# Layer one in fp32 for its first three tiles, experts' weights split two ahead, and their rows turned by TensorE

## The chip, the cores and the metric

The kernel runs on one core of one Trainium2 chip. The metric is the device time of the whole launch in microseconds. Matrix products run on TensorE (PE in the profile, its weight loads PEld), element-wise work on VectorE (DVE), ScalarE (ACT) and GpSimd (POOL), and most DMAs are issued by SyncE's queue (SP), some by GpSimd's.

## What is computed

Windowed attention feeds a two-layer block, and its result feeds eight experts with a greedy assignment of tokens. All inputs are given as float64. Cut to what matters:

```python
scores = scale * q @ k.T                  # (4, 8, 576, 64), window of 64 keys
attn = softmax(where(mask, scores, -1e9))
x = rearrange(attn @ v)                   # 2304 tokens x 512

h = x @ w_in                              # 512 x 2048: "layer one"
g = where(h > 0, h, exp(min(h, 0)) - 1)   # ELU
x = g @ w_out                             # 2048 x 512: "layer two"

logits = x @ w_gate                       # 8 experts
# all 2304 x 8 logits in falling order: a token goes to the first expert
# that still has room; each expert takes exactly 288 tokens
out[mask_e] = maximum(x[mask_e] @ w1[e], 0) @ w2[e]   # 512 -> 1024 -> 512
```

## The kernel before

Most products need more than f16 gives, so an operand is **split**: `hi` is its f16 rounding, `lo` the f16 of the rest, and a product of two split operands is three f16 products (hi hi, hi lo, lo hi). The attention's products and the transposes run in fp32.

The weights W_in and W_out come as float64. `to32` (L103) joins the two 32-bit halves with three integer operations on VectorE (L106 to L108) into a float32, and then splits it: ScalarE writes `hi` and VectorE `lo` (L115, L116), or, in every other call, ScalarE scales and writes `hi`, and GpSimd `lo` (L111 to L113). `prep_win` (L140) does that for W_in in 16 pieces into `wi`, `prep_wout` for W_out in 16 pieces.

Attention goes in 18 chunks of 128 tokens. `att_s1` turns q and k by TensorE, `att_s2` makes the scores, `att_soft` the exponentials and their normalising (L289, one GpSimd operation per half chunk), `att_s3` turns the result, and `att_s4` multiplies by v: L303 takes `vn`, the chunk's own rows, and `vp`, rows shifted by 64. `vp` is written by GpSimd (L241, L243) for chunks 0 to 5, and loaded once more from HBM for the rest (L222, L223). `att_out` puts the result, split (L315 ScalarE, L316 VectorE), into `xt`, the input of layer one.

Layer one runs over seven tiles of 256, 256, 256, 256, 512, 512 and 256 tokens (`layer1`, L361). A step takes 512 results: for tiles of 256 tokens that is 2 x 12 products of 256 columns (L377). ELU is then a chain: ScalarE relu and exp (L381, L382), GpSimd (L383), VectorE with the accumulator (L384), GpSimd `hi` (L386), VectorE `lo` (L387; on GpSimd in tile 0). The three accumulator banks `mm` come free with L384. Layer two (`layer2`, L434) takes 48 products of 512 columns for 128 tokens. Streams are interleaved by `weave` with estimated weights, and the framework's scheduler then orders each engine's instructions by a timeline of its own. Layer one of tiles 0 to 2, attention's first chunks and the preparing of both weights come first; layer two of tile 0 starts after them.

From about 440 us the routing runs, a chain of small steps between VectorE and TensorE in seven phases. Its TensorE instructions are pinned in program order, and between them stand products of layer two of tiles 4, 5 and 6 as a filling: the table `W` says how many at which step (`W[7]` and `W[8]` once per phase, `W[15]` once ahead of the first phase, whose first product is L599).

Then the experts run one after the other. Expert e has 96 + 96 products of 288 columns (L864, L899) on 288 tokens, which GpSimd gathers and SP's transposing DMAs turn (`xet`). ScalarE writes `hi` of the first products (`finish`, L869), VectorE `lo` (L870). The weights of expert e come in four pieces of 1 MB (`raw`, three buffers, SP). `split_expert` splits them: `hi` on ScalarE (L769) and GpSimd (L771), `lo` on VectorE (L772). Experts 0 and 1 are split during routing, expert e + 1 during expert e from e = 1 on. The results leave split into `oh` (`leave`), three DMA transposes per expert on SP turn them (`rt`, L826), ScalarE and VectorE join them to `orow`, and GpSimd scatters the rows to the output. Only the last expert is turned by TensorE (`last_rows`, L851).

Of the kernel before, what the change touches and what calls it, by code (L numbers as in the profile page):

```python
# [39 lines left out]
def attention_moe_moe2_kernel(ctx: ExitStack, tc: tile.TileContext, q, k, v, w_in, w_out, w_gate, w1, w2, out):  # L40
# [119 lines left out]
    def prep_wout(j):  # L160
        for f in range(4 * j, 4 * j + 4):
# [6 lines left out]
            to32(st, 64.0, w[:, 0, i], w[:, 1, i], f % 2 == 0)  # L168
# [56 lines left out]
    CV = 6  # L225

    def att_s1(c):
# [12 lines left out]
        elif c < CV:  # L240
            nc.gpsimd.tensor_scalar(VP[c][64:], V[c - 1][64:], 1.0, 1.0, op0=OP.mult, op1=OP.mult)  # L241
        if c < CV:
            nc.gpsimd.tensor_scalar(VP[c][:64], V[c][:64], 1.0, 1.0, op0=OP.mult, op1=OP.mult)  # L243
# [33 lines left out]
    def att_soft(c):  # L277
# [10 lines left out]
        for blk in range(2):  # L288
            nc.gpsimd.tensor_tensor(P[c, blk], P[c, blk], rs[:, blk, :, None].to_broadcast([128, ND, 128]), op=OP.mult)  # L289
# [71 lines left out]
    def layer1(t, pools=None):  # L361
# [5 lines left out]
        for f in range(0, NF, nf):  # L367
# [12 lines left out]
            r = work.tile([128, nf, n], F32, name="r", bufs=3)  # L380
# [660 lines left out]
```

## Time and profile before

| what | us |
|---|---|
| median of three timed runs | 840.78 (839.29 to 842.84) |
| profiled execution | 838.07 |
| its span | 836.4 |
| TensorE busy in the span | 749.8 (90%) |
| VectorE busy | 454.6 (54%) |
| ScalarE busy | 342.2 (41%) |
| GpSimd busy | 362.2 (43%) |

The profile shows one execution. A busy share is a mean over stages with different limits, so the span is read in stages: 0 to 39 the first loads and chunks, 39 to 169 layer one of tiles 0 to 2 with attention and both weights, 169 to 440 layer two and the rest of attention and layer one, 440 to 603 routing, and from there the experts. A timeline row's length of a run of products runs to the end of its last, which overlaps the next row; spacing is read from the starts.

### The profile page before, as it was taken

How to read it: one execution, taken by the hardware profiler on the slowest of the kernel's cores; microseconds unless marked ns; L12 is line 12 of the kernel's file. 1: busy time of each engine (PE TensorE's matmuls, PEld its weight loads, DVE VectorE, ACT ScalarE, POOL GpSimd, SP SyncE). 2: the span in 40 equal slices, each digit the busy share in tenths (PEclk: the TensorE clock that was granted, in tenths of full speed). 3: DMA queues.
4: the chain of work that ended last, by engine and by line, in shares of the span. 5: the costliest groups of instructions: out<-in, count | busy, mean ns of one | idle time of the engine just before them, and what ended most of it. 6: DMA issues, size and time to landing. Idle time of an engine off the chain costs nothing.

```text
span 836.4 us, 16758 instructions
## 1 busy us (share of the span) xinstructions
PE 749.8 (90%) x6742; PEld 489.7 (59%) x6742; DVE 454.6 (54%) x980; ACT 342.2 (41%) x847; POOL 362.2 (43%) x474
## 2 busy tenths in 40 slices
PE   7578878899999999999997899798879988898996
PEld 5466666645685456555583344343457766676786
DVE  4777899821164115455546655756613675457550
ACT  4666556524454246644446611301112234333332
POOL 7357475623242124575447522825061444433321
PEclk9799889999999999999998999999989999999998
DMA  9956364405456536010104220400044789988831
GB/s 238 309 122 171 96 151 138 90 1 127 102 102 121 108 92 87 1 52 1 44 14 162 99 77 18 171 14 13 25 116 90 228 211 272 254 238 187 255 89 39
DMA packets 156669, 98.82 MB, mean 118 GB/s; under 512 B 135600, under 2 KB 135600, under 8 KB 156592
## 3 DMA queue, kind: packets, MB, share of 16 engines
q1 hardware_dynamic: 153520, 88.31, 41.9%
q0 software_dynamic: 3072, 9.44, 3.9%
q8 instruction: 53, 0.87, 0.4%
q14 instruction: 24, 0.20, 0.1%
HBM read 72.37 MB, written 9.44 MB: 98 GB/s over the span
## 4 chain that ended last, share of the span: by engine, by line
PE 49%; DVE 22%; DMA 11%; issue 7%; ACT 4%; POOL 3%; SPq 3%; POOLq 0%; ACTq 0%; DVEq 0%
PE ps_mm L434 19%; PE ps_mm L377 16%; DMA raw<-in_moe_w_dram 7%; PE ps_mm L864 3%; DVE b L107 2%; DVE slab L772 2%; DVE b L106 2%; DMA out_dram<-orow,idx 2%; DVE b L108 2%; ACT sm L284 2%; PE ps_pv L303 2%; DVE r L384 1%; PE ps_sc L599 1%; DVE ge L596 1%; SPq L208 1%
## 5 line engine op out<-in xcount | busy, mean ns | idle before, releaser
L377 PE MATMUL ps_mm<-xt,slab 128*128 128x256 f16 (+1 forms) x1344 | 207.1, 313 | 15.4 <-DVE r L384 12.8
L434 PE MATMUL ps_mm<-slab,g 128*128 128x512 f16 x864 | 216.4, 384 | 0.0
L377 PEld LDWEIGHTS <-slab 128*128 128x128 f16 x1344 | 132.1, 101 | 74.1 <-issue 15.2
L434 PEld LDWEIGHTS <-g 128*128 128x128 f16 x864 | 74.5, 99 | 75.9 <-issue 8.5
L864 PE MATMUL ps_mm<-xet,slab 128*128 128x288 f16 (+1 forms) x840 | 104.2, 282 | 7.8 <-DVE h L870 7.0
L864 PEld LDWEIGHTS <-slab 128*128 128x128 f16 x840 | 77.9, 100 | 29.9 <-issue 9.9
L899 PEld LDWEIGHTS <-slab 128*128 128x128 f16 x960 | 79.1, 98 | 27.3 <-issue 10.2
L899 PE MATMUL ps_sc<-h,slab 128*128 128x288 f16 (+1 forms) x480 | 72.8, 263 | 9.1 <-ACT h L869 9.1
L381 ACT ACTIVATE r<-ps_mm 128x512 f32<-128x512 f32 x72 | 42.9, 598 | 90.7 <-PE ps_mm L377 59.8
L384 DVE TENSOR_TENSOR r<-ps_mm,r 128x512 f32<-128x512 f32 x72 | 49.6, 689 | 53.1 <-POOL r L383 53.0
L383 POOL TENSOR_SCALAR r<-r 128x512 f32<-128x512 f32 x72 | 53.7, 746 | 54.3 <-ACT r L382 49.9
L289 POOL TENSOR_TENSOR sm<-sm,rs 128x512 f32<-128x512 f32 x36 | 39.8, 1126 | 86.1 <-DVE rs L287 41.2
L386 POOL TENSOR_SCALAR g<-r 128x512 f16<-128x512 f32 x72 | 50.5, 702 | 57.2 <-DVE r L384 38.9
L899 PE MATMUL ps_tp<-h,slab 128*128 128x288 f16 (+1 forms) x480 | 71.7, 263 | 0.0
L772 DVE SCALAR_TENSOR_TENSOR slab<-raw,slab 128x512 f16<-128x512 f32 x96 | 64.5, 706 | 7.7 <-ACT slab L769 4.0
L387 DVE TENSOR_TENSOR g<-r,g 128x512 f16<-128x512 f32 x64 | 46.6, 729 | 38.9 <-POOL g L386 38.5
L816 POOL DMA_INDIRECT out_dram<-orow,idx x24 | 31.9, 1329 | 73.2 <-DVE orow L839 57.1
L284 ACT ACTIVATE sm<-ps_sc,mx 128x128 f32<-128x128 f32 x144 | 50.8, 378 | 26.1 <-DVE mx L282 26.1
L769 ACT ACTIVATE slab<-raw 128x512 f16<-128x512 f32 x48 | 27.5, 621 | 73.6 <-DMA raw<-in_moe_w_dram 72.7
L447 POOL TENSOR_TENSOR xs<-r,xs 128x512 f16<-128x512 f32 x17 | 21.0, 1233 | 68.1 <-ACT xs L446 68.1
L445 ACT ACTIVATE r<-ps_mm 128x512 f32<-128x512 f32 x17 | 10.2, 601 | 98.1 <-PE ps_mm L434 98.1
L771 POOL TENSOR_SCALAR slab<-raw 128x512 f16<-128x512 f32 x48 | 29.7, 633 | 43.2 <-DMA raw<-in_moe_w_dram 38.0
(212 smaller groups left out, 1145.6 us busy)
## 6 DMA issues: line engine op xcount, KB each, us to landing
raw<-in_moe_w_dram SPq DMA_DIRECT2D x32, 1024.0 KB, 5.4
slab<-in_moe_w_in_dram SPq DMA_DIRECT2D x16, 512.0 KB, 7.2
st<-in_moe_w_out_dram SPq DMA_DIRECT2D x16, 512.0 KB, 4.6
x2d<-xs SPq DMA_DIRECT2D x18, 256.0 KB, 2.1
qn<-in_q_dram SPq DMA_DIRECT2D x16, 256.0 KB, 6.5
kn<-in_k_dram SPq DMA_DIRECT2D x16, 256.0 KB, 6.1
vn<-in_v_dram SPq DMA_DIRECT2D x16, 256.0 KB, 4.9
vp<-in_v_dram SPq DMA_DIRECT2D x24, 128.0 KB, 3.1
```

Of the source, the lines that this page charges most:

```text
L284: nc.scalar.activation(P[c, blk][:, i], SC[blk][:, i], AF.Exp, bias=mx[:, blk, i:i + 1], accum_out=rs[:, blk, i:i + 1])
L289: nc.gpsimd.tensor_tensor(P[c, blk], P[c, blk], rs[:, blk, :, None].to_broadcast([128, ND, 128]), op=OP.mult)
L377: nc.tensor.matmul(ph[:, i], wi[d, (f + i) // 8][:, a, (f + i) % 8 * 128:((f + i) % 8 + 1) * 128], XT[t][:, b, d, :n], start=m == 0, stop= ...
L381: nc.scalar.activation(r, ph, AF.Relu, scale=-1.0 / A_H)
L383: nc.gpsimd.tensor_scalar(r, r, -1.0, A_H, op0=OP.add, op1=OP.mult)
L384: nc.vector.tensor_tensor(r, ph, r, op=OP.max)
L386: last["pool"] = nc.gpsimd.tensor_scalar(hi, r, 1.0, 1.0, op0=OP.mult, op1=OP.mult).ins
L387: (nc.gpsimd if t < 1 else nc.vector).tensor_tensor(g[:, f % fg:f % fg + nf, 1], r, hi, op=OP.subtract)
L434: pe(nc.tensor.matmul(px, g[:, f % fg, a, 128 * i:128 * i + 128], wo[f // 2][:, b, f % 2, :], start=m == 0, stop=m == 3 * NF - 1))
L772: dv(nc.vector.scalar_tensor_tensor(t[:, 1, c], st[:, g], 64.0, t[:, 0, c], op0=OP.mult, op1=OP.subtract))
L864: nc.tensor.matmul(ph[:, r], W1[e][d][:, a, f * 128:(f + 1) * 128], XET[e][:, b, d, r], start=m == 0, stop=m == 3 * ND - 1)
L899: nc.tensor.matmul(po[:, :n], w[:, a, f % 2, d * 128:(d + 1) * 128], H2[e][:, b, f, r], start=m == 0, stop=m == 3 * NF2 - 1)
```

## The change

**Layer one, tiles 0 to 2.** `prep_win` only converts W_in, into unsplit float32 slabs `wi32`. A step of these tiles is 2 x 4 fp32 products of 256 columns with an unsplit `xt`. `att_out` there is one ScalarE copy. The ELU has ScalarE relu and exp, one VectorE operation with the accumulator, and the split on ScalarE and VectorE. W_in is split (`split_win`) in the stretch of layer two of tile 0, for tiles 3 to 6.

**No GpSimd arithmetic in this stage.** All splits are ScalarE and VectorE; normalising is eight VectorE operations per chunk; `vp` is copied from `vn` by DMAs on SP (35 where 24 from HBM were).

**Routing.** The filling starts with the first chunk of tile 4, then tile 6, and three numbers of `W` are raised.

**Experts.** During expert e the weights of expert e + 2 are split, from e = 0 on. Results leave by one ScalarE copy to `oT` in fp32, 12 fp32 transposes per expert turn them, and a ScalarE copy makes `orow`.

```diff
-    def to32(st, scale, dst_hi, dst_lo, pool=False):
+    def to32(st, b):
         u, l = st[:, :, 1], st[:, :, 0]
-        b = w64.tile([128, 512], U32, name="b", bufs=3)
...
-        if pool:
-            nc.scalar.activation(v, v, AF.Copy, scale=scale)
-            nc.scalar.activation(dst_hi, v, AF.Copy)
-            nc.gpsimd.tensor_tensor(dst_lo, v, dst_hi, op=OP.subtract)
...
+    def split(v, scale, dst_hi, dst_lo):
+        nc.scalar.activation(dst_hi, v, AF.Copy, scale=scale)
+        nc.vector.scalar_tensor_tensor(dst_lo, v, scale, dst_hi, op0=OP.mult, op1=OP.subtract)
...
-            to32(win_st[i, d], 32.0, w[:, 0, c], w[:, 1, c], d % 2 == 0)
+            to32(win_st[i, d], wi32[d, i // 2][:, (i % 2) * 512:(i % 2 + 1) * 512])
             yield 600
+
+    def split_win():
+        for h in range(2):
+            for d in range(ND):
+                wi[d, h] = slab([128, 2, DF // 2])
+                v = wi32[d, h].bitcast(F32)
+                for c in (slice(0, 512), slice(512, 1024)):
+                    split(v[:, c], 32.0, wi[d, h][:, 0, c], wi[d, h][:, 1, c])
+                yield 1
...
-            if c >= CV:
-                nc.sync.dma_start(VP[c][:64], rows(v, 128 * c, 64))
-                nc.sync.dma_start(VP[c][64:], rows(v, 128 * c - 64, 64))
+            nc.sync.dma_start(VP[c][:64], V[c][:64])
+            if c:
+                nc.sync.dma_start(VP[c][64:], V[c - 1][64:])
...
-            nc.gpsimd.tensor_tensor(P[c, blk], P[c, blk], rs[:, blk, :, None].to_broadcast([128, ND, 128]), op=OP.mult)
+            for i in range(ND):
+                nc.vector.tensor_scalar(P[c, blk][:, i], P[c, blk][:, i], rs[:, blk, i:i + 1], None, op0=OP.mult)
...
+        if t < NF32:
+            if j == 0:
+                XT[t] = xtp.tile([128, ND, TILES[t]], F32, name="xt", tag="xt")
+            nc.scalar.activation(XT[t][:, :, r], px, AF.Copy)
+            return
...
+    NF32 = 3
...
+            if t < NF32:
+                for i in range(nf):
+                    c = slice((f + i) % 8 * 128, (f + i) % 8 * 128 + 128)
+                    for d in range(ND):
+                        nc.tensor.matmul(ph[:, i], wi32[d, (f + i) // 8].bitcast(F32)[:, c], XT[t][:, d, :n],
+                                         start=d == 0, stop=d == ND - 1)
+                nc.scalar.activation(r, ph, AF.Relu, scale=-1.0)
+                nc.scalar.activation(r, r, AF.Exp, scale=-1.0)
+                nc.vector.scalar_tensor_tensor(r, r, -1.0, ph, op0=OP.add, op1=OP.max)
+                split(r, A_H, hi, lo)
+                yield 16 * 512 / 2.4
+                continue
...
     def o_rows(e):
-        def turn(j):
-            rt = moe.tile([128, 2, ND, 128], F16, name="rt", bufs=RB)
-            nc.sync.dma_start_transpose(out=rt.rearrange("p a d n -> p (a d) n"),
-                                        in_=OH[e % 2][:, j].rearrange("p a d n -> p (a d n)"))
-            return rt
...
-    def last_rows(e):
         for j in range(3):
             po = bank("pv", 1, [128, ND, 128])
             for d in range(ND):
...
-                if e == E - 1:
-                    nc.scalar.activation(OT[e][:, d, r], po[:, :n], AF.Copy, scale=2.0 ** -18)
-                else:
...
+                nc.scalar.activation(OT[e][:, d, r], po[:, :n], AF.Copy, scale=2.0 ** -18)
...
-    weave((layer2(0), UT), attend(A1, A1 + 2))
+    weave((layer2(0), UT), attend(A1, A1 + 2), (split_win(), 8.5))
...
-    W = [1, 4, 2, 5, 0, 2, 5, 3, 8, 4, 16, 2, 6, 4, 2, 9, 3]
+    W = [1, 4, 2, 5, 0, 2, 5, 6, 11, 4, 16, 2, 6, 4, 2, 28, 3]
...
-        for i, _ in enumerate(chain(layer2(6), layer2(4), layer2(5))):
+        for i, _ in enumerate(chain(layer2(4, [0]), layer2(6), layer2(4, [1, 2, 3]), layer2(5))):
...
-        ss.append((chain(*([split_expert(e + 1)] if 0 < e < E - 1 else []), *([xe_t(e + 1)] if e < E - 1 else [])), 9400.0))
+        sp = split_expert(e + 2) if e < E - 2 else iter(())
+        ss.append((chain(take(sp, 8 if e < E - 2 else 0), xe_t(e + 1) if e < E - 1 else iter(()), sp), 9400.0))
```

**VectorE, in the first stage, where the third chunk is normalised.** `slab` on the right is a float64 piece of W_in, `b` the joined value. Before:

```order
L286 TENSOR_SCALAR rs<-rs 128x8
L287 RECIPROCAL rs<-rs 128x8
L106 TENSOR_SCALAR b<-slab 128x512
L107 SCALAR_TENSOR_TENSOR b<-slab,b 128x512
L316 SCALAR_TENSOR_TENSOR xt<-ps_pv,xt 128x4x128
L108 SCALAR_TENSOR_TENSOR b<-slab,b 128x512
L116 SCALAR_TENSOR_TENSOR slab<-b,slab 128x512
L106 TENSOR_SCALAR b<-slab 128x512
L107 SCALAR_TENSOR_TENSOR b<-slab,b 128x512
L108 SCALAR_TENSOR_TENSOR b<-slab,b 128x512
L116 SCALAR_TENSOR_TENSOR slab<-b,slab 128x512
L282 TENSOR_REDUCE mx<-ps_sc 128x4 x2
```

After, at the same place (L105 to L107 are the three joining operations, L292 the normalising, L284 the maximum of the next chunk):

```order
L288 TENSOR_SCALAR rs<-rs 128x8
L289 RECIPROCAL rs<-rs 128x8
L292 TENSOR_SCALAR sm<-sm,rs 128x128 x8
L105 TENSOR_SCALAR slab<-slab 128x512
L106 SCALAR_TENSOR_TENSOR slab<-slab 128x512
L105 TENSOR_SCALAR slab<-slab 128x512
L107 SCALAR_TENSOR_TENSOR slab<-slab 128x512
L106 SCALAR_TENSOR_TENSOR slab<-slab 128x512
L284 TENSOR_REDUCE mx<-ps_sc 128x4 x2
```

The splits of W_in and of `xt` (L116, L316) are gone from between the conversions, and eight normalising operations stand where two instructions on GpSimd were.

**TensorE, at the end of the same stage,** where the kernel after has its last products of layer one (L388) among scores of a chunk (L271 to L276), ahead of layer two's first (L455):

```order
L388 MATMUL ps_mm<-xt,slab 128x256 x16
L276 MATMUL ps_sc<-kt,qt 64x64 x2
L273 MATMUL ps_sc<-kt,qt 64x64 x2
L388 MATMUL ps_mm<-xt,slab 128x256 x8
L271 MATMUL ps_sc<-kt,qt 64x128 x2
L276 MATMUL ps_sc<-kt,qt 64x64 x2
L388 MATMUL ps_mm<-xt,slab 128x256 x16
L273 MATMUL ps_sc<-kt,qt 64x64 x2
L388 MATMUL ps_mm<-xt,slab 128x256 x16
L271 MATMUL ps_sc<-kt,qt 64x128 x2
L388 MATMUL ps_mm<-xt,slab 128x256 x16
L455 LDWEIGHTS g
```

Before, layer two's first product follows 48 products of L377 in a row, and one chunk more of attention stands ahead of it.

**TensorE, inside an expert** (L857 is the first product of an expert, 96 of them, `ps_pv` the bank of the turned rows). Before, weight loads and products alternate there with nothing between them. After:

```order
L857 LDWEIGHTS slab
L857 MATMUL ps_mm<-xet,slab 128x288
L844 MATMUL ps_pv<-ident,oT 96x128
L857 LDWEIGHTS slab
L857 MATMUL ps_mm<-xet,slab 128x288
L857 LDWEIGHTS slab
L857 MATMUL ps_mm<-xet,slab 128x288
L844 MATMUL ps_pv<-ident,oT 96x128
L857 LDWEIGHTS slab
L857 MATMUL ps_mm<-xet,slab 128x288
L857 LDWEIGHTS slab
L857 MATMUL ps_mm<-xet,slab 128x288
```

One transpose of the former expert's result stands between every two products for a while; two more groups of four follow later in the same expert.

**SP, over two experts.** Before, transposes of results (`rt<-oh`) and of tokens (`xet<-xe`) stand between the loads of raw weights:

```order
L826 DMA_TRANSPOSE rt<-oh_7296 128x8x128 x2
L748 DMA raw<-in_moe_w_dram 128x4x512
L826 DMA_TRANSPOSE rt<-oh_7296 128x8x128
L745 DMA raw<-in_moe_w_dram 128x2x1024
L803 DMA_TRANSPOSE xet<-xe 128x8x96
L745 DMA raw<-in_moe_w_dram 128x2x1024
L803 DMA_TRANSPOSE xet<-xe 128x8x96
L748 DMA raw<-in_moe_w_dram 128x4x512
L803 DMA_TRANSPOSE xet<-xe 128x8x96
L826 DMA_TRANSPOSE rt<-oh_7295 128x8x128 x2
L748 DMA raw<-in_moe_w_dram 128x4x512
L826 DMA_TRANSPOSE rt<-oh_7295 128x8x128
```

After:

```order
L766 DMA raw<-in_moe_w_dram 128x2x1024
L769 DMA raw<-in_moe_w_dram 128x4x512 x2
L766 DMA raw<-in_moe_w_dram 128x2x1024
L824 DMA_TRANSPOSE xet<-xe 128x8x96 x3
L766 DMA raw<-in_moe_w_dram 128x2x1024
L769 DMA raw<-in_moe_w_dram 128x4x512 x2
L766 DMA raw<-in_moe_w_dram 128x2x1024
L824 DMA_TRANSPOSE xet<-xe 128x8x96 x3
```

The transposes of results are gone, and the three of tokens stand in a row behind four loads.

## Rows read from the trace of the kernel before

**Rows 1.** the page: its first line

```profile
span 836.4 us, 16758 instructions
```

**Rows 2.** windows by stage: busy us of each engine, granted clock, DMA share

```profile
0.00:39.00 39.00, 25.04 (x256) 17.46 (x257) 21.86 (x36) 21.93 (x72) 20.32 (x58) 0.89 1.07 269
39.00:169.00 130.00, 107.47 (x1121) 85.19 (x1121) 110.47 (x152) 75.88 (x193) 80.60 (x81) 0.89 0.51 131
169.00:440.00 271.00, 270.63 (x2583) 163.50 (x2582) 106.75 (x224) 124.01 (x327) 103.36 (x150) 1.00 0.32 67
```

**Rows 3.** TensorE lines, 39 to 169: busy us, mean ns, idle before

```profile
L377 PE MATMUL ps_mm<-xt,slab 128*128 128x256 f16 x576 | 76.0, 295 | 15.1 <-DVE r L384 12.4 <-ACT slab L115 1.2 <-DVE slab L116 0.8
```

**Rows 4.** windows of experts 1 to 6: the first two and the sum

```profile
641.60:665.10 23.50, 23.50 (x194) 18.78 (x192) 16.16 (x30) 6.39 (x15) 6.34 (x6) 1.00 0.64 163
665.10:692.30 27.20, 24.02 (x194) 18.76 (x192) 16.71 (x31) 10.34 (x24) 11.81 (x14) 1.00 0.93 242
...
sum 161.50, PE 146.94 PEld 114.15 DVE 99.87 ACT 57.99 POOL 63.60; mean PE 24.49 PEld 19.02 DVE 16.64 ACT 9.66 POOL 10.60
```

**Rows 5.** waits, 641 to 803: us in total, times, longest us

```profile
ACT slab L769 <- DMA raw<-in_moe_w_dram: 72.7, 21, 7.3
...
PE ps_sc L899 <- ACT h L869: 7.4, 5, 2.4
...
PE ps_mm L864 <- DVE h L870: 7.0, 6, 2.3
```

**Rows 6.** timeline of TensorE, routing: start us, us, [idle before]

```profile
454.44 0.58 PE L599 MATMUL ps_sc<-C,ge 128*96 128x24 bf16 x6 [5.80 <-DVE C L568]
```

**Rows 7.** timeline of TensorE: stage one, and at full clock

```profile
87.77 4.59 PE L377 MATMUL ps_mm<-xt,slab 128*128 128x256 f16 x24
...
168.94 3.40 PE L434 MATMUL ps_mm<-slab,g 128*128 128x512 f16 x15
...
222.41 2.78 PE L377 MATMUL ps_mm<-xt,slab 128*128 128x256 f16 x24
225.03 0.60 PE L231 MATMUL ps_tp<-ident,qn 128*128 128x128 f32 x4
225.47 0.60 PE L236 MATMUL ps_tp<-ident,kn 128*128 128x128 f32 x4
```

**Rows 8.** lines of the whole run, nearest in kind

```profile
L303 PE MATMUL ps_pv<-pt,vp 128*64 128x64 f32 x288 | 14.3, 234 | 0.0
...
L286 DVE TENSOR_SCALAR rs<-rs 128x8 f32<-128x8 f32 x18 | 3.5, 192 | 24.0 <-ACT sm L284 24.0
...
L851 PE MATMUL ps_pv<-ident,oT 128*96 128x128 f32 x12 | 2.3, 281 | 0.7 <-ACT oT L905 0.6
...
L553 DVE TENSOR_SCALAR logits<-logits,ab 128x144 f32<-128x144 f32 x1 | 0.4, 382 | 0.0
```

**Rows 9.** VectorE by line, 0 to 169

```profile
L116 DVE SCALAR_TENSOR_TENSOR slab<-b,slab 128x512 f16<-128x512 f32 x16 | 16.7, 1042 | 2.7 <-ACT slab L115 2.7
...
L107 DVE SCALAR_TENSOR_TENSOR b<-st,b 128x512 uint32<-128x512 uint32 x16 | 15.2, 964 | 0.0
...
L106 DVE TENSOR_SCALAR b<-slab 128x512 uint32<-128x512 uint32 x16 | 11.5, 718 | 1.6 <-DMA slab<-in_moe_w_in_dram 1.5
```

**Rows 10.** instructions of L107 and L106 up to 169: duration ns min/median/max

```profile
L107 DVE SCALAR_TENSOR_TENSOR b<-slab,b x16: 640/694/1527, 12.2 to 89.6; 128x512 uint32<-128x512 uint32 x16
...
L106 DVE TENSOR_SCALAR b<-slab x16: 394/420/1382, 11.8 to 88.3; 128x512 uint32<-128x512 uint32 x16
```

**Rows 11.** TensorE by line, 169 to 440

```profile
L434 PE MATMUL ps_mm<-slab,g 128*128 128x512 f16 x398 | 91.4, 379 | 0.0
L377 PE MATMUL ps_mm<-xt,slab 128*128 128x512 f16 x384 | 86.8, 379 | 0.4 <-DVE r L384 0.4
L377 PE MATMUL ps_mm<-xt,slab 128*128 128x256 f16 x385 | 44.6, 272 | 0.0
L294 PE MATMUL ps_tp<-ident,sm 128*128 128x128 f32 x84 | 13.0, 278 | 0.0
```

More of the change, by code (lines that the diff above doesn't have):

```diff
@@ L138, in attention_moe_moe2_kernel @@
     wl = chain(*(load_win(i) for i in range(4)))
+    wi32 = {}
     def prep_win(i):
@@ L167, in prep_wout @@
             nc.sync.dma_start(st.rearrange("p n t -> p (n t)"), w_out[f * 128:(f + 1) * 128, :].bitcast(U32))
-            to32(st, 64.0, w[:, 0, i], w[:, 1, i], f % 2 == 0)
+            b = w64.tile([128, 512], U32, name="b", bufs=3)
+            to32(st, b)
+            split(b.bitcast(F32), 64.0, w[:, 0, i], w[:, 1, i])
             yield 1
@@ L239, in att_s1 @@
             nc.gpsimd.memset(VP[c][64:], 0.0)
[L240 to L243, printed above, removed]
     SC = {}
@@ L372, in layer1 @@
             ph = bank("mm", 3, [128, nf, n])
+            r = work.tile([128, nf, n], F32, name="r", bufs=3)
+            hi, lo = (g[:, f % fg:f % fg + nf, a] for a in range(2))
+            if t < NF32:
[10 more added lines that the diff above has]
+                continue
             for i in range(nf):
@@ L379, in layer1 @@
                         m += 1
-            r = work.tile([128, nf, n], F32, name="r", bufs=3)
             nc.scalar.activation(r, ph, AF.Relu, scale=-1.0 / A_H)
@@ L384, in layer1 @@
             nc.vector.tensor_tensor(r, ph, r, op=OP.max)
-            hi = g[:, f % fg:f % fg + nf, 0]
             last["pool"] = nc.gpsimd.tensor_scalar(hi, r, 1.0, 1.0, op0=OP.mult, op1=OP.mult).ins
-            (nc.gpsimd if t < 1 else nc.vector).tensor_tensor(g[:, f % fg:f % fg + nf, 1], r, hi, op=OP.subtract)
+            nc.vector.tensor_tensor(lo, r, hi, op=OP.subtract)
             yield 12 * 512 / 2.4
@@ L807, in attention_moe_moe2_kernel @@
     spacer = consts.tile([1, 1], F32)
-    RB = 2
-    RL = 2
-    RO = 0
     def scatter(e, j, orow):
@@ L823, in o_rows @@
     def o_rows(e):
-        def turn(j):
-            rt = moe.tile([128, 2, ND, 128], F16, name="rt", bufs=RB)
-            nc.sync.dma_start_transpose(out=rt.rearrange("p a d n -> p (a d) n"),
-                                        in_=OH[e % 2][:, j].rearrange("p a d n -> p (a d n)"))
-            return rt
-        rts = [turn(j) for j in range(RB)]
-        for _ in range(RL):
-            yield 450
-        for j in range(3):
-            if len(rts) == j:
-                rts.append(turn(j))
-            rt = rts[j]
-            orow = moe.tile([G, DM], F32, name="orow")
-            nc.scalar.activation(orow, rt[:G, 0].rearrange("p d n -> p (d n)"), AF.Copy, scale=2.0 ** -6)
-            st = nc.vector.scalar_tensor_tensor(orow, rt[:G, 1].rearrange("p d n -> p (d n)"), 2.0 ** -6, orow,
-                                              op0=OP.mult, op1=OP.add)
-            if RO:
-                dv(st)
-            scatter(e, j, orow)
-            yield 450
-    def last_rows(e):
         for j in range(3):
@@ L889, in expert @@
             yield 1475
-        if e == E - 1:
-            OT[e] = moe.tile([128, ND, CAP], F32, name="oT", bufs=1)
+        OT[e] = moe.tile([128, ND, CAP], F32, name="oT")
         for r in [slice(j * G, j * G + G) for j in range(3)] if e == E - 1 else [slice(0, CAP)]:
@@ L996, in attention_moe_moe2_kernel @@
     ordered.append(1)
-    OH = [moe.tile([128, 3, 2, ND, 128], F16, name=f"oh{n}", bufs=1) for n in range(2)]
-    for t in OH:
-        nc.vector.memset(t[:, :, :, :, G:], 0.0)
     for e in range(E):
         if e == E - 1:
-            tail = last_rows(e)
+            tail = o_rows(e)
         ss = [(expert(e, xe_first() if e == 0 else None, tail if e == E - 1 else None), 24000.0)]
```

23 lines of the change are left out of this document (5 added, 18 removed).

## The prediction

> **What bounds the kernel now.** I read the windows of each stage first, then the waits of TensorE in the stages where it is not full, then the rows that price what is added. The span is 836.4 us [rows 1] and the profiled execution took 838.07, so 1.67 us lie around it; the median of the three timed runs is 840.78, which is 2.7 above the profiled one. All sums are made against 838.07, and 2.7 is added at the end.
>
> TensorE sets the end nearly everywhere, but with holes in two places that the change touches. From 39 to 169 us it works 107.5 of 130 us at a granted clock of 0.89, while VectorE works 110.5 of the same 130 [rows 2]. All 576 products of layer one's first three tiles lie in this stretch, and 15.1 us of idle stand right before them, 12.4 of it until VectorE's L384 has freed the accumulator [rows 3]. From 169 to 440 TensorE is full, 270.63 of 271 us [rows 2]: there only TensorE's own work counts, and what moves in on other engines is hidden. From 641.6 to 803.1, experts 1 to 6, it works 146.94 of 161.50 us; the first of these windows, in which no weights are split, is full at 23.50 of 23.50, the next takes 27.20 [rows 4]. There TensorE waits 7.4 us for ScalarE's L869 and 7.0 for VectorE's L870 [rows 5], because those two also split the next expert's weights; ScalarE itself stands 72.7 us waiting for raw weights at the head of its queue [rows 5]. In the first step of routing one hole of 5.80 us stands before L599 [rows 6].
>
> **Stage one: TensorE's side.** A run of 24 products of 256 columns takes 222.41 to 225.03, so 0.109 us each; four fp32 operations of 128 columns take 225.03 to 225.47, so 0.11 each [rows 7]. The trace shows no fp32 product of 256 columns. L303 holds 144 fp32 products for each operand in the code, and its row counts 288 [rows 8]: two passes each. Bounds: one pass of 2 x 0.11 = 0.22 us, or two, 0.44. L303 is the nearest kind, so I take 0.437. Removed: 576 x 0.109 = 62.8. Added: 192 x 0.437 = 83.9. TensorE gets 21.1 us more work, and with nothing else changed that is a loss.
>
> **Stage one: the other side.** VectorE works 21.86 + 110.47 = 132.3 us up to 169 [rows 2], so it idles 36.7. The 96 integer operations that join the float64 halves stand in six rows, 80.4 us together, of which the longest and the shortest are shown [rows 9]; quiet medians are 0.420 for L106 and 0.694 for L107 [rows 10], L108 being of L107's form, so quiet they cost 32 x (0.42 + 0.69 + 0.69) = 57.6. The rest, 22.8, I put down to GpSimd's arithmetic beside it, which leaves this stage. The 16 splits of L116 take 1.042 instead of about 0.69 [rows 9], 5.6 more; as many stay, W_out's, while W_in's move to the full stretch. VectorE takes over the normalising: eight operations of 128 columns a chunk, about seven chunks. No row has that shape; 8 columns take 0.192 and 144 take 0.382 [rows 8], while 512 take 0.42 when quiet [rows 10]. So the 0.382 is contended, and a line from 0.192 to 0.42 gives 0.24: 56 x 0.24 = 13.4, with 10.8 and 21.4 as ends. The new ELU has 48 VectorE operations for 24 steps in place of 35: 13 x 0.69 = 9.0. Six L316 go: 4.1. VectorE's sum is 132.3 - 22.8 - 5.6 + 13.4 + 9.0 - 4.1 = 122.2; with the same idle, layer two starts at 158.9.
>
> TensorE's own path says much the same. The seventh step, the first that needs W_in's last quarter, starts at 87.77 [rows 7]; without the split behind the conversion I take 84. Then 18 steps of 8 x 0.437 = 62.9, and about two chunks of attention. A chunk costs 4.5 us at full clock: of the 270.63, 398 + 384 products of 512 columns at 0.218 take 170.5, 385 of 256 take 42.0, some 450 tiny gate products about 12, which leaves 46 to 48 for 10.5 chunks, eight L294 each [rows 11]. So 84 + 62.9 + 9 = 156. Both engines are near full at once, so I take **160** for layer two's first product instead of 168.94 [rows 7]: 8.9 us gained. The order puts about one chunk less ahead of that product (208 score products of L271's kind against 240). This chunk goes to the full stretch: -4.5. Stage one: **+4.4** net; with 172 and 147 as ends of the start, -7.5 to +17.4. Moved to that stretch at no cost: W_in's 16 + 16 split operations, covered by 270.63 us of TensorE work; if TensorE had to wait for wi before tile 3, they would cost up to 16 x 0.69 = 11.
>
> The SBUF-to-SBUF copies of v wait on SP for v's landing, and loads of q, k and weights are queued behind them. They run some two chunks ahead of use, so I cost them at nothing; without that lead see rival F.
>
> **Routing.** 61 layer-two products, at 0.218, move earlier. 19 of them, 4.1 us, stand where the hole of 5.80 us is: free. Three more at each of two places in six phases are partly covered: with six phases and 1.3 us of added work in each, I take half as exposed, 4 us. The last phase is left unfilled, and gives back the 13.3 us of products as far as they stood in the chain's way. I take about 5, since its chain also runs on VectorE. **+1**, ends -3 and +5.
>
> **Experts.** Weights split two ahead are ready earlier, and three DMA transposes per expert go. TensorE gets 12 fp32 transposes per expert, 12 x 0.109 = 1.3 us (84 in all, 9.2 us). At best each of six windows is 23.5 + 1.3 = 24.8: 148.8 against 161.50, a gain of 12.7. I leave 3.9 of waits, as ScalarE still has the raw weights' splits ahead of L869's kind in its queue; and expert 7 pays 1.3 for expert 6's rows. **+7.5**, ends +2 and +11.4. Behind the new waits for raw on SP stand only loads of later experts.
>
> A single transpose, not followed by its like, lasts 0.281 us by L851 [rows 8], while four in a row come 0.11 apart [rows 7]. The Trainium skill, page "TensorE: Matmul & The Clock Gate", section "Part 4: PE-mode transpose", gives about 275 ns for a transpose in a kernel's context, which speaks against turning rows on TensorE. The trace agrees for the duration and not for the spacing; by the page's figure the sum would be 84 x 0.275 = 23 us instead of 9.2, and the time about 842.
>
> **The sum.** 838.07 - 4.4 - 1 - 7.5 = 825.2; with 2.7, **828 us**.
>
> **The rivals.** B, slower: stage one's holes are not VectorE's contention but attention's own chain and late loads, so they stay while the products grow. Then +21.1 with 8.5 gained elsewhere: 850.7, or 853. It decides from a first layer-two product later than 168.94 + 8.5 - 4.5 = 173 us. For it speaks that TensorE is busy 83% of that stretch already; against it the 12.4 us that end with L384 and the medians of [rows 10].
> C: the experts' waits stay, since ScalarE's queue holds splits of still later raw weights ahead of what frees the accumulator; TensorE pays 9.2 on top. The 72.7 us [rows 5] speak for it; against it the earlier start. 838.07 - 5.4 + 9.2 = 841.9, or 844.6.
> D: each transpose holds TensorE its 0.281 us: 84 x (0.281 - 0.109) = 14.4 more: 839.6, or 842. Most stand one at a time between two products, which speaks for it.
> E, better: VectorE's relief is whole, and layer two starts at 148: 12 us more than forecast, 813.2, or 816.
> F: the copies of v hold SP; in the full stretch the transposing loads of wt and x2t come late and TensorE stands about 10 us: 838.
> That fp32 products are chosen and then run as one pass would be E's case too.
>
> **How the numbers follow.** Forecast 0.53 (own range 821 to 836), B 0.14, C 0.09, D 0.06, E 0.13, F 0.05. The range 814 to 842 leaves out B, half of C and the far end of E. Half a per cent, 4.2 us, is what a measurement of this kernel can tell from no change: 836.6 to 845. Faster: forecast and E, a little of F, 0.68. The same: C, D, F and the forecast's upper edge, 0.15. Slower: B and the worst of C, 0.17.
>
> **What would show it.** Layer two's first product near 160; the fp32 product's two passes 0.22 apart; L105 to L107 near 0.42, 0.69, 0.69; a granted clock above 0.89 from 39 to 169; the hole before the first L599 near 1.7; expert windows near 25 with a DMA share under 0.9; transposes 0.11 apart. I am wrong in stage one if TensorE's waits end with W_in's conversion instead, in the experts if windows stay near 27.

## The result, and the profile after

The kernel after takes 852.31 us (848.55 to 854.41, four runs) where the kernel before takes 840.33: a ratio of 1.0133, 95% interval 1.0084 to 1.0182. It is slower, by 12 us. Forecast was 828, range 814 to 842.

The profiled execution of after took 854.41, its span is 852.6. Read by the first products of each stage, the two kernels stand like this (us from the span's start):

| | before | after | difference |
|---|---|---|---|
| layer one's first product | 39.2 | 32.5 | -6.7 |
| layer two's first product | 168.9 | 152.0 | -16.9 |
| routing's first product of L547 (after: L568) | 444.7 | 435.3 | -9.4 |
| first product of the experts | 612.4 | 605.3 | -7.1 |
| end of span | 836.4 | 852.6 | +16.2 |

At the experts' first product after is 7.1 us ahead; from there to the end it loses 23.3. Windows of after by stage (us, then busy us of TensorE, its weight loads, VectorE, ScalarE, GpSimd, then granted clock, DMA share, GB/s), to lay beside [rows 2]:

```profile
0.00:39.00 39.00, 27.89 (x286) 20.58 (x287) 24.49 (x66) 18.73 (x65) 6.62 (x44) 0.96 1.09 267
39.00:152.00 113.00, 105.02 (x791) 85.20 (x791) 84.94 (x176) 66.66 (x165) 0.00 (x0) 0.98 0.60 154
152.00:435.00 283.00, 280.31 (x2767) 170.14 (x2765) 140.02 (x339) 144.59 (x377) 79.40 (x127) 1.00 0.32 70
435.00:605.00 170.00, 143.77 (x887) 65.38 (x886) 105.46 (x350) 43.57 (x78) 74.89 (x94) 0.90 0.20 69
```

In stage one from 39 us on, the granted clock is 0.98 instead of 0.89, TensorE works 105.02 of 113 us, and GpSimd not at all. The windows of experts 1 to 6, beside [rows 4]:

```profile
634.20:665.00 30.80, 26.94 (x206) 20.91 (x204) 12.94 (x24) 9.00 (x22) 9.43 (x13) 0.94 0.61 184
665.00:698.10 33.10, 28.04 (x207) 21.60 (x206) 13.00 (x24) 10.43 (x24) 12.33 (x16) 0.90 0.62 190
698.10:732.70 34.60, 27.98 (x206) 21.49 (x204) 13.18 (x24) 10.30 (x23) 11.92 (x16) 0.90 0.67 185
...
762.00:794.10 32.10, 27.60 (x207) 21.39 (x205) 12.99 (x24) 9.98 (x24) 8.87 (x11) 0.89 0.57 149
794.10:818.90 24.80, 24.80 (x207) 20.15 (x205) 3.66 (x8) 6.44 (x16) 2.75 (x3) 1.00 0.09 25
sum 184.70, PE 160.68 PEld 125.55 DVE 68.64 ACT 56.22 POOL 54.93; mean PE 26.78 PEld 20.93 DVE 11.44 ACT 9.37 POOL 9.15
```

Sum 184.7 against 161.5. Expert 6, in which no weights are split any more, is full: 24.80 of 24.80, which is just 23.5 + 1.3. Six such windows would be 148.8. The other 35.9 us are of two kinds: TensorE stands 184.7 - 160.68 = 24.0 us, and it works 160.68 instead of 148.8, that is 11.9 more at a granted clock down to 0.89. The DMA share is about 0.6 in the first five. The waits in this stretch (us, times, longest), beside [rows 5]:

```profile
ACT slab L790 <- DMA raw<-in_moe_w_dram: 81.1, 18, 7.3
...
PE ps_pv L844 <- ACT oT L896: 15.7, 4, 5.1
...
PE ps_sc L891 <- ACT h L862: 6.2, 3, 3.0
```

The wait before L844, the transposes of result rows, was not there before. One such place on TensorE:

```profile
665.03 2.00 PE L857 MATMUL ps_mm<-xet,slab 128*128 128x288 f16 x15
672.10 0.45 PE L844 MATMUL ps_pv<-ident,oT 128*96 128x128 f32 x1 [5.06 <-ACT oT L896]
672.34 0.69 PE L857 MATMUL ps_mm<-xet,slab 128*128 128x288 f16 x2
672.82 0.42 PE L844 MATMUL ps_pv<-ident,oT 128*96 128x128 f32 x1
...
674.42 3.81 PE L857 MATMUL ps_mm<-xet,slab 128*128 128x288 f16 x15
678.02 0.37 PE L891 MATMUL ps_sc<-h,slab 128*128 128x288 f16 x1
```

From 665.03 it does 15 products of expert 2, then waits 5.06 us for the copy `oT` of expert 1's result; and it comes back at half the clock, two products from 672.34 to 672.82, 0.24 each where the 15 from 665.03 on came 0.12 apart, until about 678. The granted clock from 672 to 678 is 0.50. ScalarE in the same time:

```profile
664.09 1.15 ACT L790 ACTIVATE slab<-raw 128x512 f16<-128x512 f32 x2 [6.49 <-DMA raw<-in_moe_w_dram]
670.60 1.15 ACT L790 ACTIVATE slab<-raw 128x512 f16<-128x512 f32 x2 [5.36 <-DMA raw<-in_moe_w_dram]
671.65 0.39 ACT L896 ACTIVATE oT<-ps_sc 128x288 f32<-128x288 f32 x1
...
672.53 0.42 ACT L896 ACTIVATE oT<-ps_tp 128x288 f32<-128x288 f32 x1
675.40 1.15 ACT L790 ACTIVATE slab<-raw 128x512 f16<-128x512 f32 x2 [2.45 <-DMA raw<-in_moe_w_dram]
676.46 0.39 ACT L862 ACTIVATE h<-ps_mm 128x288 f16<-128x288 f32 x1
```

ScalarE stands 6.49 and 5.36 us until raw weights land, splits them, and only then makes the four copies (L896) that TensorE waits for; the first eviction of the next expert's products (L862) stands behind one more pair of splits. These weights belong to an expert two further on. The loads themselves on SP, and VectorE:

```profile
658.06 0.37 SPq L766 DMA_DIRECT2D raw<-in_moe_w_dram  x1
658.54 5.74 SPq L824 DMA_TRANSPOSE xet<-xe  x3
664.45 0.45 SPq L766 DMA_DIRECT2D raw<-in_moe_w_dram  x1
665.07 15.91 SPq L769 DMA_DIRECT2D raw<-in_moe_w_dram  x2
689.46 0.37 SPq L766 DMA_DIRECT2D raw<-in_moe_w_dram  x1
```

```profile
658.20 4.90 DVE L793 SCALAR_TENSOR_TENSOR slab<-raw,slab 128x512 f16<-128x512 f32 x8
676.88 0.46 DVE L863 SCALAR_TENSOR_TENSOR h<-ps_mm,h 128x288 f16<-128x288 f32 x1 [13.78 <-ACT h L862]
677.25 1.28 DVE L793 SCALAR_TENSOR_TENSOR slab<-raw,slab 128x512 f16<-128x512 f32 x2
...
679.79 0.68 DVE L793 SCALAR_TENSOR_TENSOR slab<-raw,slab 128x512 f16<-128x512 f32 x1
```

Raw weights have three buffers. The second load of L769's pair is issued some 15 us after the first, since its buffer comes free with the last of four of VectorE's `lo` halves (L793, from 677.25 to 680.47), and these stand in order behind L863 at 676.88, which waits for L862, which waits for the weights' splits on ScalarE. So the loads wait for the evictions and the evictions wait for the loads.

### The profile page after: what moved, and what is told of

Read it like the earlier page. It is cut to its first block, busy times and chain, and to the rows that moved or that the text cites. A ratio compares the mean times of both kernels' runs of the same rounds, so it can differ in the third digit from the quotient of the medians.

```text
span 852.6 us, 16465 instructions
## 1 busy us (share of the span) xinstructions
PE 771.8 (91%) x6634; PEld 514.0 (60%) x6634; DVE 440.7 (52%) x1091; ACT 346.2 (41%) x855; POOL 234.7 (28%) x355
## 4 chain that ended last, share of the span: by engine, by line
PE 56%; DMA 17%; DVE 10%; issue 9%; ACT 3%; POOL 2%; SPq 2%; POOLq 0%; ACTq 0%; DVEq 0%
PE ps_mm L455 19%; PE ps_mm L400 13%; DMA raw<-in_moe_w_dram 12%; PE ps_mm L388 8%; DMA slab<-in_moe_w_in_dram 3%; PE ps_mm L857 2%; PE ps_pv L306 2%; DVE slab L793 2%; PE ps_tp L297 1%; DVE ge L617 1%; PE ps_sc L620 1%; DMA wt<-slab 1%; POOL out_dram L833 1%; DMA st<-in_moe_w_out_dram 1%; DVE D L611 1%
## 5 line engine op out<-in xcount | busy, mean ns | idle before, releaser
L455 PE MATMUL ps_mm<-slab,g 128*128 128x512 f16 x864 | 212.8, 383 | 0.0
L400 PE MATMUL ps_mm<-xt,slab 128*128 128x256 f16 (+1 forms) x768 | 130.7, 326 | 1.3 <-DVE r L406 1.3
L455 PEld LDWEIGHTS <-g 128*128 128x128 f16 x864 | 75.4, 99 | 72.4 <-issue 1.7
L857 PE MATMUL ps_mm<-xet,slab 128*128 128x288 f16 (+1 forms) x840 | 113.9, 293 | 4.3 <-issue 2.1
L863 DVE SCALAR_TENSOR_TENSOR h<-ps_mm,h 128x288 f16<-128x288 f32 x64 | 29.2, 456 | 138.3 <-ACT h L862 138.2
L400 PEld LDWEIGHTS <-slab 128*128 128x128 f16 x768 | 72.4, 98 | 46.8 <-issue 1.9
L857 PEld LDWEIGHTS <-slab 128*128 128x128 f16 x840 | 82.4, 105 | 25.5 <-issue 4.8
L891 PEld LDWEIGHTS <-slab 128*128 128x128 f16 x960 | 78.8, 98 | 23.7 <-issue 6.9
L388 PE MATMUL ps_mm<-xt,slab 128*128 128x256 f32 x384 | 89.1, 388 | 1.1 <-DVE slab L107 1.1
L388 PEld LDWEIGHTS ps_mm<-xt,slab 128*128 128x128 f32 x384 | 72.3, 192 | 13.2 <-DVE slab L107 1.4
L286 ACT ACTIVATE sm<-ps_sc,mx 128x128 f32<-128x128 f32 x144 | 50.8, 379 | 34.5 <-DVE mx L284 34.4
L790 ACT ACTIVATE slab<-raw 128x512 f16<-128x512 f32 x48 | 27.6, 621 | 91.2 <-DMA raw<-in_moe_w_dram 89.9
L793 DVE SCALAR_TENSOR_TENSOR slab<-raw,slab 128x512 f16<-128x512 f32 x96 | 61.7, 685 | 0.0
L403 ACT ACTIVATE r<-ps_mm 128x512 f32<-128x512 f32 x48 | 28.8, 600 | 63.7 <-PE ps_mm L400 56.0
L405 POOL TENSOR_SCALAR r<-r 128x512 f32<-128x512 f32 x48 | 34.0, 707 | 51.7 <-ACT r L404 50.9
L408 DVE TENSOR_TENSOR g<-r,g 128x512 f16<-128x512 f32 x48 | 34.3, 716 | 26.4 <-POOL g L407 26.3
L406 DVE TENSOR_TENSOR r<-ps_mm,r 128x512 f32<-128x512 f32 x48 | 33.0, 689 | 27.7 <-POOL r L405 27.7
```

What stands on the lines that cost most here:

```text
L286: nc.scalar.activation(P[c, blk][:, i], SC[blk][:, i], AF.Exp, bias=mx[:, blk, i:i + 1], accum_out=rs[:, blk, i:i + 1])
L388: nc.tensor.matmul(ph[:, i], wi32[d, (f + i) // 8].bitcast(F32)[:, c], XT[t][:, d, :n], start=d == 0, stop=d == ND - 1)
L400: nc.tensor.matmul(ph[:, i], wi[d, (f + i) // 8][:, a, (f + i) % 8 * 128:((f + i) % 8 + 1) * 128], XT[t][:, b, d, :n], start=m == 0, stop= ...
L405: nc.gpsimd.tensor_scalar(r, r, -1.0, A_H, op0=OP.add, op1=OP.mult)
L406: nc.vector.tensor_tensor(r, ph, r, op=OP.max)
L408: nc.vector.tensor_tensor(lo, r, hi, op=OP.subtract)
```

## The experiments

Each ratio is to the kernel before on the same chip; its medians there were 836.6 to 843.0. "Routing" is routing's first product and "experts" the time from the experts' first product to the last, both from the profiled execution. Runs stand on several chips, so kernels of different chips are compared by their ratios.

| run | after, but | us | ratio (95%) | routing | experts |
|---|---|---|---|---|---|
| before | | 840.3 | 1 | 444.7 | 215.6 |
| after | | 852.3 | 1.013 (1.008 to 1.018) | 435.3 | 239.9 |
| e1 | before's expert stage | 830.1 | 0.988 (0.981 to 0.996) | 435.6 | 218.6 |
| e2 | rows turned by DMA | 843.3 | 1.007 (1.004 to 1.009) | 434.5 | 233.2 |
| e3 | weights one ahead | 843.4 | 1.007 (1.003 to 1.010) | 436.5 | 229.5 |
| e4 | old filling and `W` | 850.0 | 1.016 (1.009 to 1.023) | 433.6 | 235.6 |
| m1 | all `hi` halves on GpSimd | 815.6 | 0.975 (0.970 to 0.981) | 432.2 | 203.0 |
| m2 | raw loads of a quarter | 816.4 | 0.976 (0.971 to 0.980) | 435.8 | 202.8 |
| m3 | rows turned later | 845.6 | 1.011 (1.005 to 1.017) | 433.7 | 230.5 |
| m4 | e3, rows turned later | 836.6 | 1.000 (0.997 to 1.002) | 434.2 | 222.9 |
| n1 | e1 with m1's edit | 828.4 | 0.983 (0.978 to 0.989) | 435.2 | 213.9 |
| b1 | before with m1's edit | 841.7 | 1.000 (0.996 to 1.003) | 445.3 | 220.1 |
| s1 | m1, normalising on GpSimd | 809.8 | 0.962 (0.957 to 0.967) | 429.5 | 202.3 |
| s2 | m1 without fp32 | 814.7 | 0.967 (0.963 to 0.972) | 432.9 | 204.0 |
| r1 | m1 with e4's edit | 815.6 | 0.969 (0.964 to 0.974) | 433.7 | 203.0 |
| t1 | s1, eight W_out splits on GpSimd | 811.3 | 0.963 (0.958 to 0.967) | 430.6 | 204.8 |
| t2 | s1 without fp32 | 811.7 | 0.964 (0.959 to 0.969) | 432.8 | 200.9 |

Eleven of these kernels (after, e1 to e4, m1 to m4, n1, r1) have the same stages ahead of routing, and it starts between 432.2 and 436.5 in them: differences of 2 us there tell nothing.

**Which part of the experts.** e1 takes before's whole expert stage, e2 only its DMA transposes and split results, e3 only its splitting one ahead:

```diff
-        sp = split_expert(e + 2) if e < E - 2 else iter(())
-        ss.append((chain(take(sp, 8 if e < E - 2 else 0), xe_t(e + 1) if e < E - 1 else iter(()), sp), 9400.0))
+        ss.append((chain(*([split_expert(e + 1)] if 0 < e < E - 1 else []), *([xe_t(e + 1)] if e < E - 1 else [])), 9400.0))
```

> The kernel after with the whole expert stage of the kernel before (weights one expert ahead, rows turned by DMA). After has 226.6 us from the first L857 to the last, before had 202.7, and everything ahead of the experts ends 7.1 us earlier in after. If the loss lies in the experts alone: about 840.3 - 7 = 833, or 852.3 - 23.9 = 828. If part of the loss is carried in from the stages ahead: 838 or more.

> The kernel after, but results leave split and are turned by DMA transposes as before; the weights stay split two ahead. Theory T1 (transposes stand in TensorE's queue and wait for results that ScalarE copies only behind splits of late raw weights; 15.7 us of waits before L844): the waits go, 830 to 836. Theory T2 (the order of splitting two ahead starves the loads of raw weights, 89.9 us of ScalarE waits, and everything in order waits for them): 847 or more.

> The kernel after, but weights split one ahead in the place that before has; rows stay turned by TensorE. T1: the waits before L844 stay, 846 or more. T2: the raw weights flow as in before, 828 to 836.

The loss is in the experts: e1 is faster than before. Of T1 and T2 neither holds alone: each half of the change loses 13 us on e1, on the same chip, and both together 21 (by the ratios, 0.988 and 1.013). The two halves stop TensorE at different places: in e3 it waits 15.4 us for the copies `oT`, in e2 14.4 for VectorE's `lo` ahead of the second products.

**The routing table**, put back in e4 and, on top of m1's edit, in r1:

> The kernel after with the filling order and the three numbers of W of before. From the first L568 to the first expert product after takes 170.0 us, before (L547) 167.7. If the new table costs this 2.3 us: 850. If it gives the 1 us of the prediction: 853.

> The kernel after with hi halves on GpSimd in the experts (815.6), and the filling order and the three numbers of W of before. By the spans of the first group of runs (168.7 against 169.3 to 170.0 from routing's start to the first expert product): 814 to 815.6. By the prediction: 816.6.

Neither shows a difference: from routing's start to the experts' first product takes 168.7 and 170.0 with the old table, and 168.4 to 170.0 with the new one.

**ScalarE's queue, the loads, the place.** m1 takes the splits of experts 2 to 7 off ScalarE, m2 makes the loads small (it leaves out three quarters of the weights), m3 and m4 move the transposes:

```diff
-                        if g % 2:
-                            nc.scalar.activation(t[:, 0, c], st[:, g], AF.Copy, scale=64.0)
-                        else:
-                            nc.gpsimd.tensor_scalar(t[:, 0, c], st[:, g], 64.0, 1.0, op0=OP.mult, op1=OP.mult)
+                        nc.gpsimd.tensor_scalar(t[:, 0, c], st[:, g], 64.0, 1.0, op0=OP.mult, op1=OP.mult)
```

> The kernel after with all hi halves of the experts' weights (from expert 2 on) written by GpSimd, none by ScalarE: what ScalarE evicts no longer stands behind a split that waits for raw weights. Theory H (head of ScalarE's queue: L896 and L862 wait behind L790): the 15.7 us of waits before L844 and some of those before L891 go, 832 to 840. Rival S (the supply of raw weights itself, three buffers that VectorE's ordered lo halves release late, sets the pace whichever engine waits): 847 or more.

> The kernel after with a quarter of every raw load of experts 2 to 7 (512 of 2048 columns are loaded, and the splits read these four times): same instructions on all compute engines, 256 KB in place of 1 MB, so the weights of these experts are not the reference's. Both H and S hold that late raw weights are the root: ScalarE's 89.9 us of waits fall, expert windows come to about 25 us, 826 to 832. If instead the transposes on TensorE and the order cost the time by themselves: 845 or more.

```diff
     def o_rows(e):
+        if e < E - 1:
+            yield 1000
         for j in range(3):
```

> The kernel after with the turning of a finished expert's rows put off to about the middle of the next expert (weights still two ahead). If the 15.7 us before L844 come from where the transposes stand: they go, 838 to 842, since the other half of the loss (two ahead) stays. If TensorE pays for the 84 transposes wherever they stand: 850 or more.

> Weights one ahead as before, and rows turned by TensorE about the middle of the next expert. If place is all: the 13 us that rows on TensorE cost in the run with one ahead go but for the 9.2 us or less that the transposes take: 830 to 836. If not: 843 as there.

m1 gains more than H asked for, about 32 us on after by the ratios (0.975 and 1.013), and with full loads is as fast as m2 with a quarter of them. So the supply of weights was never short in itself; it was short because its buffers hung on ScalarE's queue. The waits for raw at the head of that queue are not a cost by themselves: in m2 they still add up to 50.8 us, and in m1 ScalarE stands 45.1 us for buffers of `orow` instead, without TensorE losing by it. What TensorE still waits for in m1's experts, and the windows of its expert 2 and of experts 1 to 6 together:

```profile
PE ps_mm L854 <- DVE h L860: 1.5, 3, 0.9
...
PE ps_sc L888 <- ACT h L859: 0.2, 1, 0.2
```

```profile
651.40:676.30 24.90, 24.90 (x207) 20.22 (x206) 14.20 (x24) 6.42 (x16) 18.40 (x21) 1.00 0.87 241
...
sum 151.60, PE 149.77 PEld 121.02 DVE 80.10 ACT 38.19 POOL 96.01; mean PE 24.96 PEld 20.17 DVE 13.35 ACT 6.36 POOL 16.00
```

Expert 2 is full at full clock, and over the six TensorE stands 151.60 - 149.77 = 1.8 us. In m3 TensorE no longer waits for the copies `oT`, but it waits before L893, the second products, which need ScalarE's `hi`, and 5.6 us for the transposes' own bank; ScalarE stands 82.5 us for raw weights, where in after it is 89.9:

```profile
ACT slab L790 <- DMA raw<-in_moe_w_dram: 82.5, 21, 8.7
...
PE ps_sc L893 <- ACT h L864: 12.1, 5, 3.0
```

m3's 845.6 lies between its two expectations, and m4 is quicker than e3 by 6.8 us (before took 836.8 and 836.6 beside them), where 7 to 13 were expected. So the place of the transposes is worth a part (experts 230.5 for 239.9), and the rest of the wait moves to another place.

**Is it the edit or the change?** n1 gives the edit of m1 to e1, b1 to the kernel before:

> The kernel after with the whole expert stage of before (one ahead, rows by DMA) and there, too, all hi halves of experts 2 to 7 on GpSimd. Theory H says that every wait of that stage hung on ScalarE's queue: 817 to 822 from 830. If two ahead and rows on TensorE are worth something by themselves once ScalarE's queue is free, it stays behind the 815.6 of the run with them, by up to 7; if they are worth nothing, the two are equal.

> The kernel before with one edit: all hi halves of experts 2 to 7 on GpSimd. The run with before's expert stage behind after's other stages had its expert stage go from 218.6 to 213.9 us with the same edit: 832 to 838 where before has 838 to 843, 0.5% less.

With the old expert stage the edit gives 0.5% (n1) or nothing (b1), less than was expected of either: H does not explain that stage. With two ahead and rows on TensorE it gives 3.7%. Then the new stage is worth 10.9 us against n1's (203.0 and 213.9; r1 and n1, on one chip, are 815.6 and 828.4): a good change, whose gain needs a free ScalarE queue. What the old stage still waits for, with the splits off ScalarE, stands in n1's waits:

```profile
ACT orow L856 <- DMA rt<-oh: 30.4, 12, 7.0
...
DVE orow L857 <- ACT orow L856: 27.7, 8, 6.0
...
PE ps_mm L882 <- DVE h L888: 11.4, 6, 4.3
```

TensorE's longest stop there, 4.3 us, ends with an L888 that starts at 698.56 right behind an L857. That one joins turned rows and stands behind ScalarE's L856, which waited 7.0 us for the rows' DMA transpose. This is the same kind of blocking with another load at the head; in m1, where TensorE turns the rows, it is gone.

**Stage one.** s1 puts normalising back on GpSimd, t1 also eight of W_out's splits; s2 (from m1) and t2 (from s1) have no fp32.

```diff
-            for i in range(ND):
-                nc.vector.tensor_scalar(P[c, blk][:, i], P[c, blk][:, i], rs[:, blk, i:i + 1], None, op0=OP.mult)
+            nc.gpsimd.tensor_tensor(P[c, blk], P[c, blk], rs[:, blk, :, None].to_broadcast([128, ND, 128]), op=OP.mult)
```

```diff
+            b = w64.tile([128, 512], U32, name="b", bufs=3)
+            to32(win_st[i, d], b)
+            split(b.bitcast(F32), 32.0, wi[d, i // 2][:, 0, c], wi[d, i // 2][:, 1, c])
...
-    NF32 = 3
+    NF32 = 0
```

> The kernel after with hi halves on GpSimd in the experts (815.6), and attention's normalising back on GpSimd, two operations a chunk. P (stage one was quicker than forecast because VectorE is rid of GpSimd's arithmetic beside it): layer two's first product from about 150 to 158 or later, and longer integer operations on VectorE. Q (because fp32 takes the splits of W_in and of xt and GpSimd's two steps out of layer one's chain): it stays within 2 us of 150.

> The kernel after with hi halves on GpSimd in the experts (815.6), and no fp32: W_in is split in stage one by ScalarE and VectorE, tiles 0 to 2 run 12 f16 products a step with the old ELU. TensorE has 21 us less to do there. P: layer two starts earlier than 150. Q: it starts at 160 to 169 as in before, in spite of less work on TensorE.

> The best run so far (hi halves of the experts on GpSimd, normalising on GpSimd; routing starts at 429.5), with the splits of every other piece of W_out back on ScalarE twice and GpSimd, as in before: eight GpSimd operations of about 1.4 us in stage one. P2 (these GpSimd operations, which share time with VectorE's integer operations, are what cost before's stage one): L105 to L107 grow again and routing starts at 433 or later. If it is not them: 430 or earlier, since VectorE has eight splits less.

> The best run so far without fp32: W_in split in stage one by ScalarE and VectorE, 12 f16 products a step, old ELU; normalising on GpSimd. If fp32 is worth nothing in the sum (routing started at 432.9 without and 432.2 with it): the same as 429.5 within 1.5 us. If VectorE's fuller queue needs fp32 once GpSimd works beside it: 433 or later.

s1 contradicts P: layer two starts at 145.8, earlier than P and Q asked for, routing at 429.5, below the eleven others, and the median is the lowest of all. s2 contradicts Q where it matters: layer two's first product comes at 169.0, as late as in before, but routing starts at 432.9, as in m1. So the first product of layer two is a poor mark, since with fp32 more of attention is put behind it: 52 transposes of `sm` stand ahead of it in m1, 80 in s2, at eight a chunk. fp32 is worth 0 to 3 us at routing's start (432.2 against 432.9, 429.5 against 432.8), which the spread doesn't resolve; s1 and t2, on different chips, have overlapping intervals. Without fp32, s2 already has 11.8 of the gain. t1's row of the operations that run beside the GpSimd splits, and the one of the others:

```profile
L107 DVE SCALAR_TENSOR_TENSOR b<-st,b 128x512 uint32<-128x512 uint32 x16 | 12.5, 789 | 0.1
...
L107 DVE SCALAR_TENSOR_TENSOR slab<-slab 128x512 uint32<-128x512 uint32 x16 | 11.6, 732 | 0.1
```

Beside the GpSimd splits they take 0.79 (in s1, without those splits, the same rows have 0.735), and routing starts 1.1 later, less than the 3.5 that P2 asked for. What of stage one gave the 12 us (W_in's GpSimd splits, GpSimd's copies of v, or the other order that follows from them) was not separated further and stays open.

## Why the prediction was wrong

**Experts: the step that failed.** It gave +7.5, with +2 as its worst end; measured is -23.3, nearly all of it in experts 1 to 6 (184.7 us, where 152.7 was forecast and 161.5 was before). The step was "I leave 3.9 of waits, as ScalarE still has the raw weights' splits ahead of L869's kind in its queue". The wait was seen, but its 3.9 was put below the 7.4 and 7.0 us of [rows 5] without a row for it, and nothing was asked of the new instructions; TensorE stood 24.0 us and lost 11.9 more to the clock. The runs show why: the transposes add to TensorE's queue a wait for ScalarE's copies, and these copies stood behind splits of weights that are needed two experts later. Rival C named ScalarE's queue, but priced only 9.2 us of transposes and the old waits (844.6, and a chance of 0.09); it left out that TensorE's stops feed back through VectorE's order to the raw buffers, and that each stop costs the clock too (11.9 of the 35.9 us). The forecast of that stage is what it gives without ScalarE's splits: m1's windows of experts 1 to 6 are 24.8, 24.9, 25.9, 25.9, 25.3 and 24.8, 151.6 in all, where 152.7 was forecast. "Behind the new waits for raw on SP stand only loads of later experts" was true and beside the point; the waits that mattered were on ScalarE.

**Transposes.** 12 in 1.3 us was right (expert 6: 24.80 = 23.5 + 1.3), and D is out: a single one between products takes 0.24 from start to start at half clock (672.10 to 672.34), and at full clock the window leaves 0.11. The duration that the Trainium skill's page "TensorE: Matmul & The Clock Gate" (section "Part 4: PE-mode transpose") gives, about 275 ns, is again that of a row (L844's median is 273) and not its cost.

**Stage one: right sign, too small.** Layer two started at 152.0, not 160; routing 9.4 earlier, not 4.4. The prices held: an fp32 product is

```profile
145.04 7.17 PE L388 MATMUL ps_mm<-xt,slab 128*128 128x256 f32 x32
152.05 3.83 PE L455 MATMUL ps_mm<-slab,g 128*128 128x512 f16 x17
```

(152.05 - 145.04) / 16 = 0.438, 32 rows being 16 products; and VectorE's operations of stage one

```profile
L392 DVE SCALAR_TENSOR_TENSOR r<-r,ps_mm 128x512 f32<-128x512 f32 x23 | 16.0, 698 | 14.9 <-ACT r L391 14.9
...
L292 DVE TENSOR_SCALAR sm<-sm,rs 128x128 f32<-128x128 f32 x56 | 11.6, 286 | 0.1
...
L106 DVE SCALAR_TENSOR_TENSOR slab<-slab 128x512 uint32<-128x512 uint32 x16 | 10.9, 689 | 0.1
...
L105 DVE TENSOR_SCALAR slab<-slab 128x512 uint32<-128x512 uint32 x16 | 6.7, 425 | 5.4 <-DMA slab<-in_moe_w_in_dram 5.3
```

0.689 and 0.425 for the integer ones as forecast, 0.286 for a normalising one instead of 0.24. What was mis-sized is VectorE's sum up to layer two's first product: 122.2 forecast, 24.49 + 84.94 = 109.4 measured. 3.7 of the 12.8 us is a mixing of two measures. The forecast took sums of lines off a busy time of windows, and the rows of successive operations overlap (L793: eight of 0.68 in 4.90 us): by lines VectorE has 141.9 before and 122.6 after, by windows 132.3 and 109.4. Most of the rest is the new ELU, whose lines grew by 3.9 instead of 9.0 (43 of its 48 operations stand ahead of that product), and the normalising, 11.6 for 13.4. VectorE's idle time did not stay the same either: 42.6 of 152.0 us, where 36.7 was carried over.

The clock, 0.98 for 0.89, was named as a sign and not priced. Up to layer two's first product TensorE is busy 25.04 + 107.47 = 132.5 us before and 27.89 + 105.02 = 132.9 after, although its products grew by 21.1. One chunk less is 4.5 of that. The clock is about 15 by an estimate from the windows: 0.11 of 169 us was withheld before, 0.04 of 39 and 0.02 of 113 after. By this reckoning these two make up for nearly all of the 21.1, and the gain of 16.9 is idle time of TensorE, 36.5 before and 19.1 after.

Of these 16.9 us, 7.5 are given back by routing's start: 4.5 for the chunk was forecast, and TensorE stands 2.7 us of the stretch from 152 to 435, where before stood 0.4. B is out: the holes before L377 went, although the products grew by 21 us. Of 32 to 160 us this is what is left of them:

```profile
PE ps_mm L388 <- DVE slab L107: 1.1, 2, 0.8
```

F's copies of v cost no more than those 2.7. E's mechanism, VectorE's relief, was nearer for stage one, though it names neither the overlap nor the clock.

**Routing: +1 forecast, nothing shown.** The hole before the first L620 is 1.7 for 5.8 as forecast, but

```profile
PE ps_sc L620 <- DVE ge L617: 13.4, 13, 2.7
PE ps_sc L720 <- DVE rk L715: 3.6, 1, 3.6
...
PE ps_sc L620 <- DVE C L589: 1.7, 1, 1.7
```

L620's other waits are 13.4 for before's 9.5, and the last phase stands 3.6 before L720, where before stood 1.3 before L699. From routing's start to the experts takes 170.0 for 167.7, and e4 and r1 show that the table isn't the cause of a difference that can be told.

**The chances.** Slower had 0.17. The time of B, 853, was near, for a reason that has nothing to do with B.

## What to carry to other kernels

When an instruction is moved to an engine that waits in order, write out for each of its inputs what stands ahead of their producer in the producer's queue, and by what that may be held. Work for later (here, splitting weights that land some time) should not share an in-order queue with evictions that TensorE needs now: put it on an engine that nobody waits for. One edit of that kind turned 1.013 into 0.975 (0.969 in r1), and with normalising back on GpSimd it was 0.962. A wait at a queue's head is worth an edit only where something that TensorE needs stands behind it.

## What was not expected of the hardware

The price of a 5 us stop is more than the 5 us: behind it the products ran at 0.24 us instead of 0.12 for about 6 us, at a granted clock of 0.50. In experts 1 to 6 this was 11.9 us beside 24.0 of standing. And 21 us more of TensorE work in stage one cost nothing by routing's start (m1 against s2); beside it the granted clock from 39 to 150 is 0.98 in after and 1.00 in m1 with fp32 products, 0.95 in s2 with f16 ones, and 0.89 before. For after against before the clock is about 15 us by the estimate above; between m1 and s2 it was not separated.
